# GpSimd's constant operand: a row of 256 int32 in place of one int32 read with a step of zero

## The chip, the core and the metric

One NeuronCore of a Trainium2 chip runs the whole kernel. The metric is device time in microseconds (us) for one execution. The engines are called as the profile calls them: PE (TensorE; PEld its weight loads), DVE (VectorE), ACT (ScalarE), POOL (GpSimd) and SP (SyncE, which issues most of the DMAs).

## What is computed

One input x of 2048 tokens with 512 columns goes through two attention blocks of 32 heads with 16 columns each, and a gate mixes their outputs:

```python
x = A_x
g = _sigmoid((x * gate_w).sum(-1, keepdims=True))
a = _A_ref(x, A_wqkv, A_wo)     # softmax(q k^T / 4) v, then @ wo
b = _B_ref(x, B_wqkv, B_wo)     # phi(q) (phi(k)^T v) / (phi(q) sum phi(k)), then @ wo
return g * a + (1 - g) * b
```

Block A is the large part: 32 heads x 2048 x 2048 scores, an exponential of each, and a product with v (P@V) that also sums the exponentials. All of it in bf16 with fp32 accumulation, output 2048 x 512 in bf16.

## The kernel before, in words

**Tiling.** Eight heads share the 128 partitions (`NT8` = 4 groups of heads). A round is one group of heads, one chunk of 512 queries and every second head of the group, 32 rounds in all. A round has 64 units, 4 heads x 16 blocks of 128 keys; a unit is one head's scores for 128 keys x 512 queries: a matmul Q·K into a PSUM bank of 128 x 512, an exponential of it, and a P@V matmul into the bank in which the round accumulates. PE's matmuls are recorded in `pe_macro` (L685), so they all carry that line.

**Two ways to an exponential.** Most units take the first: ACT's exponential of two banks at a time from PSUM into the tile PT (L2063). The others are *claimed* (`claim`) by DVE and POOL. DVE evicts a claimed bank with one instruction (L1565), a maximum and an addition with int16 output; the integer is the bit pattern of an fp16 number that rises with the score roughly as the exponential does. To make it accurate, the kernel uses three such patterns, the second and third shifted by a constant (`STEPS` = 0, 342, 683), and lets P@V add them with weights that are multiplied into copies of v. The patterns lie in the tile DP: `NB` = 13 buffers of `NTU` = 2048 int16 a partition, each of them `NTRI` = 4 claimed units.

**The add.** When four units fill a buffer, `try_close` takes a free buffer for each of the two shifted patterns and pushes an addition of the constant. It has two forms. On DVE it is L1606: 2048 int16 plus a scalar. On POOL it is L1609: a TENSOR_TENSOR over int32, two int16 patterns at a time, 1024 int32 a partition; the second operand is the tile `steps`, which holds the constant twice in two int16, that is in one int32, for each of the two shifts:

```python
steps = SB([128, 4], I16, "step")                                             # L312
for z in range(1, NG4):                                                       # L734
    op(PO, lambda z=z: nc.gpsimd.memset(steps[:, 2 * z - 2:2 * z], STEPS[z]), writes=[r_step], dur=0.1)
...
DP[:, i2, 0:n].bitcast(I32), y, steps[:, 2 * z - 2:2 * z].bitcast(I32).to_broadcast([128, n // 2]), ALU.add))   # L1610
```

`to_broadcast` gives that one int32 a step of zero, so it is read 1024 times. The two memsets (L735) stand among POOL's first instructions, behind the zeroing of `warm` (L733) and ahead of the identity (L736, L737), the masks (L730, L740, L743) and the clearing of v's copies and of smaller tiles (L760 to L764).

**What sets the order.** The program is laid out ahead of time: a planner keeps a clock for each engine, estimates the duration of each operation (`POOL_ADD` = 1.97 us for L1609, `POOL_TT` = 1.3 us for L1294), and decides which additions go to POOL and which to DVE, and where each instruction stands in its engine's list (`pump`, `pool_go`, `emit_item_op`). The lists are then fixed; on the chip each engine works its list in order and waits on semaphores. `_emit` gives every POOL instruction one wait beyond its data: on the last DVE instruction ahead of it that has no PSUM operand, since the two engines get in each other's way at SBUF. Among those DVE instructions are L1606, L973 (a clamp of the exponentials of block B's features), L925 (the weighted copies of v), L1279 (reciprocals of the sums) and L1253 (a check of their range). POOL's only other repeated instruction is L1294, the product of P@V's output with the reciprocals, 128 x 512 fp32 twice in, bf16 out.

**Around it.** At the start a load of x is transposed by PE (L692) with the identity of L737, and the first projections follow; block B's steps and the output projection are spread between the rounds. At the end, once ACT has no more units, PE finishes the last P@V matmuls and the projection of the last 512 rows (L2154 to L2168), and the rows are stored.

Of the kernel before, what the change touches and what calls it, by code (L numbers as in the profile page):

```python
# [9 lines left out]
ALU = mybir.AluOpType  # L10
# [3 lines left out]
I32 = mybir.dt.int32  # L14
I16 = mybir.dt.int16
# [15 lines left out]
STEPS = (0, 342, 683)  # L31
# [173 lines left out]
def d_sb(n, rate=1.0):  # L205
    return 0.15 + n * 1.042e-3 * rate


def d_act(n):
    return ACT_END + n * 8.34e-4  # L210


def bass_gated_mix__mha_block__linear_attn_block__prompt_kernel(
# [33 lines left out]
    with ExitStack() as es:  # L247
        _cnt = [0]

        def SB(shape, dt, name):  # L250
            _cnt[0] += 1
            return es.enter_context(nc.sbuf_tensor(f"{name}_{_cnt[0]}", list(shape), dt))

        def SEM(name):
            return es.enter_context(nc.semaphore(name))
# [47 lines left out]
        DP = SB([128, NB, NTU], BF16, "DP")  # L303
# [5 lines left out]
        rbc = SB([128, 512], FP32, "rbc")  # L309
        dev = SB([128, 2, 128], FP32, "dev")  # L310
        flag = SB([128, 1], I32, "flag")
        steps = SB([128, 4], I16, "step")  # L312
        epool = SB([128, 2, 512], BF16, "epool")
        KVbd = SB([128, NCC, 128], BF16, "KVbd")
        Zsel = SB([128, NCC, 8], BF16, "Zsel")
# [38 lines left out]
        PO = _Eng("pool", SEM("s_pool"))  # L354
# [43 lines left out]
        r_step = R("step")  # L398
# [111 lines left out]
        def settle(reads, writes):  # L510

            while True:
                hit = None
                for it in items:
                    for k, o in enumerate(it.ops):
                        if conflicts(o, reads, writes):
                            hit = it
                            break
                    if hit:
                        break  # L520
                if hit is None:
                    return
                while True:
                    other = blocker(hit, hit.ops[0][1], hit.ops[0][2])
                    if other is None:
                        break
                    hit = other
                emit_item_op(hit)

        def _emit(E, fn, reads, writes, dur, issue=None, inc=True):  # L530
            st = est_start(E, reads, writes)
            deps = _deps_for(reads, writes)
            if E is PO:
                deps.append(port_ev[0])
            ev = E.add(fn, deps, inc=inc)
            if E is DV and not any(res in r_bank for res in reads):
                port_free[0] = st + dur - 0.03
                port_ev[0] = ev
            _record(E, ev, reads, writes)
            E.t = st + (issue if issue is not None else max(0.05, dur - 0.08))  # L540
            for res in reads:
                res.tr = max(res.tr, st + dur)
            for res in writes:
                res.tw = st + dur
                res.we = E
            return ev

        def op(E, fn, reads=(), writes=(), dur=0.2, issue=None):
            settle(reads, writes)
            return _emit(E, fn, reads, writes, dur, issue)  # L550

        def push(prio, ops):

            iseq[0] += 1
            it = _Item(prio, iseq[0], ops)
            items.append(it)
            for o in it.ops:
                for res in o[1]:
                    res.pend += 1
                for res in o[2]:  # L560
                    res.pend += 1
                    res.pw += 1
# [8 lines left out]
        def pump(now, look=0.25):  # L571
            try_close()
            pool_go()
            while items and DV.t <= now + look:
                best = None
                for it in items:
                    o = it.ops[0]
                    if len(o) == 6 or blocked(it, o[1], o[2]):
                        continue
                    if len(o) > 6 and not due_now(it) and PO.t < DV.t + POOL_WAIT:  # L580
                        continue
                    st = est_start(DV, o[1], o[2])
                    wait = st - DV.t
                    key = (wait > (WAIT_BANK if it.prio <= 1 else 0.12), -1 if it is boost[0] else it.prio, st, it.seq)
                    if best is None or key < best[0]:
                        best = (key, it, st)
                if best is None:
                    return
                if best[2] > now + look + WAIT_BANK:
                    return  # L590
                emit_item_op(best[1], False)
                pool_go()
# [98 lines left out]
        def f_tr(o, i):  # L691
# [12 lines left out]
           dur=1.6)  # L704
# [9 lines left out]
        for t in range(1, NQC):  # L714
            for cc in range(NCD):
                dma(xT[:, cc, 512 * t:512 * (t + 1)], x2[512 * t:512 * (t + 1), 128 * cc:128 * (cc + 1)], semXT[cc][t],
                    writes=[r_xT[cc][t]], total_after=16, transpose=True, E=SP, lands=5.5)
# [14 lines left out]

        op(PO, lambda: nc.gpsimd.memset(warm[:], 0.0), writes=[r_warm])  # L733
        for z in range(1, NG4):  # L734
            op(PO, lambda z=z: nc.gpsimd.memset(steps[:, 2 * z - 2:2 * z], STEPS[z]), writes=[r_step], dur=0.1)  # L735
        op(PO, lambda: nc.gpsimd.memset(identb[:], 0.0), writes=[r_ident])  # L736
        op(PO, lambda: nc.gpsimd.affine_select(out=identb[:], in_=identb[:], compare_op=ALU.not_equal,  # L737
                                               fill=1.0, base=0, pattern=[[-1, 128]], channel_multiplier=1),
# [805 lines left out]
        def free_buffers():  # L1544

            used = [e[3] for e in pv_pending]
            held_ = [c[0] for c in (tri[0], *closing) if c is not None]
            free = [i for i in range(NB) if i not in held_ and not any(x.pend or x in used for x in r_DP[i])]
            free.sort(key=lambda i: max(x.tr for x in r_DP[i]))
            return free  # L1550
# [21 lines left out]
        def add_products(i, z, k, r, u):  # L1572
            pv_pending.append((r, u, [(DP[:, i, 512 * k:512 * (k + 1)].bitcast(F16), z)], r_DP[i][k], Fraction(1, NG4)))

        def close_tri():
            if tri[0] is not None:
                closing.append((*tri[0], []))
                tri[0] = None
            try_close()
# [7 lines left out]
        def try_close():  # L1587

            while closing:
                i, us, zs = closing[0]  # L1590
                z = len(zs) + 1
                if z == NG4:
                    closing.popleft()
                    continue
                free = free_buffers()
                early = us[0][0] > acc_round[0]
                if len(free) < (LAZY if early else 1):
                    return False
                if not zs and sum(1 for it in items if it.prio == 3) >= (EARLY_ADDS if early else MOST_ADDS):
                    return False  # L1600
                i2 = free[0]
                zs.append(i2)
                n = 512 * len(us)
                y = DP[:, i, 0:n].bitcast(I16)
                mine_, out_ = r_DP[i][0:len(us)], r_DP[i2][0:len(us)]
                ops = (lambda z=z, i2=i2, y=y, n=n: nc.vector.tensor_single_scalar(DP[:, i2, 0:n].bitcast(I16), y, STEPS[z], ALU.add),  # L1606
                       mine_, out_, d_sb(n, 0.25), None)
                if n == NTU:
                    ops = (ops[0], mine_ + [r_step], out_, ops[3], None, POOL_ADD, lambda z=z, i2=i2, y=DP[:, i, 0:n].bitcast(I32), n=n: nc.gpsimd.tensor_tensor(  # L1609
                        DP[:, i2, 0:n].bitcast(I32), y, steps[:, 2 * z - 2:2 * z].bitcast(I32).to_broadcast([128, n // 2]), ALU.add))  # L1610
                push(3, [ops])
                of_round[iseq[0]] = us[0][0]
                for k, (r, u) in enumerate(us):
                    add_products(i2, z, k, r, u)
            return True
# [364 lines left out]
        while True:  # L1980
# [72 lines left out]
            for c, eb in extras:  # L2053
# [4 lines left out]
                     dur=QK_T, mac=0.053 * len(fns), mode="rows")  # L2058
            for c, eb in extras:
                claim(c[0], c[1], eb, True, in_group=True)  # L2060
            STATS["claims %d+%d" % (len(us), len(extras))] = STATS.get("claims %d+%d" % (len(us), len(extras)), 0) + 1
            n = 512 * len(us)
# [3 lines left out]
               dur=d_act(n), issue=0.055 + n * 8.34e-4)  # L2066
# [59 lines left out]
        while pv_pending:  # L2126
            if not pv_step(PE.t, force=True):
# [9 lines left out]
                 writes=[r_bank[tbank]], dur=0.3)  # L2137
# [8 lines left out]
           writes=[r_bad], dur=0.25)  # L2146
# [15 lines left out]
        for k in range(NPRE):  # L2162
# [6 lines left out]
            if k == 0:  # L2169
# [4 lines left out]
                         writes=[r_bank[tbank]], dur=0.1)  # L2174
# [47 lines left out]
        for t8 in range(NT8):  # L2222
# [11 lines left out]
            for qc in range(NQC):  # L2234
                for h in range(8):
# [6 lines left out]
                    for k in range(4):  # L2242
# [4 lines left out]
                           writes=[r_sm] + r_rdB)  # L2247
# [16 lines left out]
        for tb in range(NTB):  # L2264
            s3 = tb % NOUTT
            pe_macro(out_fns(bank_ap(tb % 4), tb, order_out), reads=[r_OT[t][tb // 4] for t in range(NT8)] + [r_OBT[tb], r_woA, r_woB],
                     writes=[r_bank[tb % 4]])
# [87 lines left out]
```

## Time and profile before

| what | value |
|---|---|
| median of 3 runs | 675.63 us (675.6 to 675.94) |
| the profiled execution, its own time | 675.2 us |
| its span, first to last instruction | 673.4 us |
| busy in the span: PE, DVE, ACT, POOL | 655.0, 576.0, 660.0, 550.8 us |
| ACT exponentials L2063 | 675, 648.1 us |
| DVE evictions L1565 of claimed units | 654, 433.0 us |
| POOL additions L1609 | 278, 527.0 us, mean 1925 ns |
| DVE additions L1606 | 50, 33.4 us |

How to read it: a row of groups names the line, the engine, the operation, the tiles written and read with their shapes, the count, the busy time and the mean duration, and then the idle time of the engine just before these instructions with what ended it. A row of waits reads "who <- for whom: us in total, times, longest". A row of windows lists for each engine the busy time in that stretch. A row of the timeline starts with the start time and the duration of a run of like instructions. Busy PE is no measure of PE's speed, since matmuls are pipelined.

### The profile page before, as it was taken

The page shows a single profiled execution, that of the slowest core. Times are in us where ns is not written, and L with a number is a line of the kernel's source. Part 1 is how long each engine was busy: PE and PEld are TensorE (multiplying, and loading weights), DVE is VectorE, ACT ScalarE, POOL GpSimd, SP SyncE. Part 2 cuts the span into 40 slices and gives each one's busy share as a digit, 9 for nine tenths or more (in the row PEclk, how much of TensorE's full clock was granted, in tenths as well). Part 3 has the DMA queues.
Part 4 walks back from the last instruction along what each step waited for, and adds up shares of the span by engine and source line. Part 5 has one row for each costly group of instructions (what it writes and reads, how often), then busy time and mean ns, then how long its engine had stood idle before and what let it go on. Part 6 is the DMA issues. An engine that isn't in the chain of part 4 may idle for free.

```text
span 673.4 us, 19207 instructions
## 1 busy us (share of the span) xinstructions
PE 655.0 (97%) x8078; PEld 200.1 (30%) x8080; DVE 576.0 (86%) x968; ACT 660.0 (98%) x715; POOL 550.8 (82%) x311
## 2 busy tenths in 40 slices
PE   8999999999999999999999999999999999999997
PEld 4322223333223232333222323323322222222223
DVE  4589889889887886888988998999889998989894
ACT  6999999999999999999999999999999999999995
POOL 5098889887889997788986999778788888898883
PEclk9999999999999999999999999999999999999999
DMA  9900101001010021101001010010211401010011
GB/s 221 252 3 12 24 2 31 6 11 27 1 35 2 18 50 35 32 2 29 7 10 35 10 41 11 16 29 13 46 26 24 52 25 42 10 44 24 20 41 44
DMA packets 44816, 22.96 MB, mean 34 GB/s; under 512 B 33976, under 2 KB 40568, under 8 KB 44728
## 3 DMA queue, kind: packets, MB, share of 16 engines
q1 hardware_dynamic: 42712, 20.12, 13.5%
q10 hardware_dynamic: 2016, 1.57, 0.9%
q8 instruction: 66, 1.08, 0.7%
q14 instruction: 22, 0.18, 0.1%
HBM read 8.00 MB, written 2.10 MB: 15 GB/s over the span
## 4 chain that ended last, share of the span: by engine, by line
ACT 95%; PE 4%; DMA 1%; DVE 1%; issue 0%; ACTq 0%
ACT PT L2063 92%; PE ps L685 3%; ACT epool L970 2%; DMA PT<-in_A_x_dram 1%; DVE DP L2165 0%; DVE xT L1909 0%; PE ps L692 0%; DVE KT L859 0%; DVE DP L2170 0%; DVE flag L2175 0%; ACT eg L954 0%; ACTq L2278 0%
## 5 line engine op out<-in xcount | busy, mean ns | idle before, releaser
L2063 ACT ACTIVATE PT<-ps 128x1024 bf16<-128x1024 f32 (+1 forms) x675 | 648.1, 1155 | 0.7 <-PE ps L685 0.5
L1609 POOL TENSOR_TENSOR DP<-DP,step 128x1024 int32<-128x1024 int32 x278 | 527.0, 1925 | 99.1 <-DVE DP L1565 27.6
L1565 DVE TENSOR_SCALAR DP<-ps 128x512 int16<-128x512 f32 x654 | 433.0, 685 | 69.1 <-PE ps L685 62.9
L685 PE MATMUL ps<-Qpad,KT 32*128 32x512 bf16 x2048 | 264.6, 384 | 10.0 <-ACT PT L2063 4.7
L685 PE MATMUL ps<-DP,Vaug 128*32 128x512 f16 x1949 | 206.8, 384 | 1.6 <-DVE oraw L1306 0.7
L685 PE MATMUL ps<-PT,Vaug 128*32 128x512 bf16 x1384 | 174.3, 384 | 0.6 <-DVE Vaug L914 0.5
L685 PEld LDWEIGHTS ps<-Qpad,KT 32*128 32x128 bf16 x2048 | 66.6, 91 | 269.9 <-ACT PT L2063 242.9
L685 PEld LDWEIGHTS ps<-DP,Vaug 128*32 128x32 bf16 x1949 | 49.7, 94 | 66.2 <-issue 41.1
L685 PEld LDWEIGHTS ps<-PT,Vaug 128*32 128x32 bf16 x1384 | 42.1, 95 | 46.7 <-issue 36.7
L685 PE MATMUL ps<-warm 128*32 128x512 bf16 (+1 forms) x272 | 46.7, 387 | 1.1 <-POOL step L735 1.1
L1606 DVE TENSOR_SCALAR DP<-DP 128x2048 int16<-128x2048 int16 (+1 forms) x50 | 33.4, 696 | 0.0
L685 PE MATMUL ps<-xT,wA 128*32 128x512 bf16 x432 | 32.6, 384 | 0.0
L1294 POOL TENSOR_TENSOR OT<-oraw,rbc 128x512 bf16<-128x512 f32 x12 | 15.6, 1302 | 11.3 <-DVE DP L1606 5.4
L970 ACT ACTIVATE epool<-ps 128x512 bf16<-128x512 f32 x32 | 23.4, 731 | 0.0
L1306 DVE COPY oraw<-ps 128x512 f32<-128x512 f32 x31 | 21.2, 682 | 0.7 <-PE ps L685 0.6
L685 PE MATMUL ps<-xT,wB 128*32 128x512 bf16 x256 | 19.7, 384 | 0.0
L685 PE MATMUL ps<-wB,xT 128*32 128x512 bf16 x256 | 19.3, 384 | 0.0
L685 PE MATMUL ps<-woA,OT 128*32 128x512 bf16 (+1 forms) x226 | 19.1, 384 | 0.0
L975 DVE SCALAR_TENSOR_TENSOR phi<-ps,epool 128x512 bf16<-128x512 f32 x24 | 16.3, 681 | 0.0
L685 PEld LDWEIGHTS ps<-warm 128*32 128x32 bf16 (+1 forms) x272 | 11.6, 98 | 13.8 <-issue 12.1
L859 DVE CAST KT<-ps 128x512 bf16<-128x512 f32 (+1 forms) x16 | 10.7, 667 | 5.2 <-PE ps L685 5.2
L685 PE MATMUL ps<-wA,xT 128*128 128x128 bf16 x192 | 14.9, 220 | 0.0
(106 smaller groups left out, 244.4 us busy)
## 6 DMA issues: line engine op xcount, KB each, us to landing
rbc<-oraw SPq DMA_DIRECT2D x16, 256.0 KB
OT<-in_A_x_dram SPq DMA_DIRECT2D x4, 512.0 KB, 7.1
Qpad<-Qs SPq DMA_DIRECT2D x124, 16.0 KB, 1.8
oraw<-oraw SPq DMA_DIRECT2D x60, 32.0 KB, 1.9
wA<-in_A_wqkv_dram SPq DMA_DIRECT2D x1, 1536.0 KB, 7.7
wB<-in_B_wqkv_dram SPq DMA_DIRECT2D x1, 1536.0 KB, 8.6
out_dram<-outt SPq DMA_DIRECT2D x12, 128.0 KB, 1.7
phi<-in_A_x_dram ACTq DMA_DIRECT2D x3, 256.0 KB, 6.1
```

The source lines that it names most:

```text
L685: return lambda: nc.tensor.matmul(o, lhsT=l, rhs=r, start=start, stop=stop, skip_group_check=sg)
L859: push(1, [(lambda: nc.vector.tensor_copy(KT[:, par, c0:c1], src), [r_bank[b]], [r_KT[par][t]], d_psum(n), None)])
L970: op(AC, lambda: nc.scalar.activation(epool[:, s, :], bank_ap(b), ACT.Exp), reads=[r_bank[b]], writes=[r_e[s]], dur=0.6, issue=0.48)
L975: (lambda: nc.vector.scalar_tensor_tensor(out=dst, in0=bank_ap(b), scalar=0.0, in1=epool[:, s, :], op0=ALU.max, op1=ALU.add), [r_bank[b], ...
L1294: push(1, [(lambda: (nc.gpsimd if on_pool else nc.vector).tensor_tensor(OT[:, t8, 512 * qc:512 * (qc + 1)], oraw[:, 0, :], rbc[:], ALU.mul ...
L1306: push(0, [(lambda: nc.vector.tensor_copy(oraw[:, half, :], acc), [r_acc], [r_oraw[half]], d_psum(512), evicted)])
L1565: push(0 if in_group else 1, [(lambda: nc.vector.tensor_scalar(DP[:, i, 512 * k:512 * (k + 1)].bitcast(I16), bank_ap(b), FRAC - Y_BIAS4, Y ...
L1606: ops = (lambda z=z, i2=i2, y=y, n=n: nc.vector.tensor_single_scalar(DP[:, i2, 0:n].bitcast(I16), y, STEPS[z], ALU.add), mine_, out_, d_sb ...
L1609: ops = (ops[0], mine_ + [r_step], out_, ops[3], None, POOL_ADD, lambda z=z, i2=i2, y=DP[:, i, 0:n].bitcast(I32), n=n: nc.gpsimd.tensor_te ...
L2063: op(AC, lambda p0=p0, b0=b0, n=n: nc.scalar.activation(PT[:, 512 * p0:512 * p0 + n], ps[:, 512 * b0:512 * b0 + n], ACT.Exp, scale=LN2 / F ...
```

## The change

The tile `steps` grows from 2 int16 to 512 int16 a partition for each of the two constants (`STEP_W` = 512), and the memsets fill all of it. The addition on POOL then reads 256 int32 of that row one after the other and begins again, four times for the 1024 elements; the patterns that it reads and writes are the same elements in the same order, only written as 4 x 256. Nothing else is edited; the form on DVE and the planner's costs stay.

```diff
-        steps = SB([128, 4], I16, "step")
+        STEP_W = 512
+        steps = SB([128, 2 * STEP_W], I16, "step")
...
-            op(PO, lambda z=z: nc.gpsimd.memset(steps[:, 2 * z - 2:2 * z], STEPS[z]), writes=[r_step], dur=0.1)
+            op(PO, lambda z=z: nc.gpsimd.memset(steps[:, STEP_W * (z - 1):STEP_W * z], STEPS[z]), writes=[r_step], dur=0.1)
...
-                        DP[:, i2, 0:n].bitcast(I32), y, steps[:, 2 * z - 2:2 * z].bitcast(I32).to_broadcast([128, n // 2]), ALU.add))
+                        DP[:, i2, 0:n].bitcast(I32).rearrange("p (a b) -> p a b", b=STEP_W // 2), y.rearrange("p (a b) -> p a b", b=STEP_W // 2),
+                        steps[:, STEP_W * (z - 1):STEP_W * z].bitcast(I32).unsqueeze(1).to_broadcast([128, n // STEP_W, STEP_W // 2]), ALU.add))
```

## The prediction

> **What bounds the kernel now.** The page comes first, for the chain that ended last; then the waits of ACT, to see whether that chain has holes; then the windows, to see where each engine stands inside and outside the long stage.
>
> ```profile
> span 673.4 us, 19207 instructions
> PE 655.0 (97%) x8078; PEld 200.1 (30%) x8080; DVE 576.0 (86%) x968; ACT 660.0 (98%) x715; POOL 550.8 (82%) x311
> ...
> ACT 95%; PE 4%; DMA 1%; DVE 1%; issue 0%; ACTq 0%
> ```
>
> ```profile
> ACT xT L1907 <- PE ps L692: 2.8, 1, 2.8
> ...
> ACT PT L2063 <- PE ps L685: 0.5, 1, 0.5
> ```
>
> ```profile
> 0.00:32.50 32.50, 29.74 (x361) 13.15 (x361) 16.44 (x33) 26.12 (x26) 8.64 (x21) 1.00 0.94 244
> 32.50:663.00 630.50, 618.80 (x7601) 182.92 (x7602) 555.03 (x924) 630.48 (x687) 542.16 (x290) 1.00 0.11 23
> 663.00:673.40 10.40, 6.50 (x120) 4.03 (x118) 4.58 (x13) 3.38 (x5) 0.00 (x0) 0.99 0.17 56
> ```
>
> The windows list PE, PEld, DVE, ACT, POOL. From 32.5 to 663 us ACT is busy 630.48 of 630.50 us, and its exponentials (L2063) waited for anything once, for 0.5 us. ACT sets the time; there is nothing in that stage to win by speeding up another engine. POOL, whose instruction the change touches, works 542.16 us of the same 630.50: it is not the bound, and has 88.3 us of idle time before it becomes one.
>
> **The edited add.** Its durations (minimum/median/maximum), a stretch of three on end, and POOL's waits:
>
> ```profile
> L1609 POOL TENSOR_TENSOR DP<-DP,step x278: 1886/1892/2397, 32.5 to 660.6; 128x1024 int32<-128x1024 int32 x139
> ```
>
> ```profile
> 639.87 5.59 POOL L1609 TENSOR_TENSOR DP<-DP,step 128x1024 int32<-128x1024 int32 x3
> ```
>
> ```profile
> POOL DP L1609 <- DVE DP L1565: 27.6, 5, 22.2
> POOL DP L1609 <- DVE epool L973: 21.7, 29, 1.4
> POOL DP L1609 <- DVE DP L1606: 14.9, 11, 2.0
> POOL DP L1609 <- DVE Vaug L925: 7.9, 5, 1.8
> ```
>
> ```profile
> L973 DVE TENSOR_SCALAR epool<-epool 128x512 bf16<-128x512 bf16 x32 | 10.3, 323 | 1.9 <-ACT epool L970 0.5
> ```
>
> There are 278 adds, nearly all at 1.89 us; on end they follow each other every (5.59 - 1.89) / 2 = 1.85 us. The instructions, their count, order and waits stay as they are: the planner's cost POOL_ADD (1.97) is not edited, so neither is anything laid out by it. What changes is how the second operand is read: now one int32 a partition, 1024 times over; afterwards 256 int32 in a row, the row four times. So the question is one price: what the add costs when its second operand moves too.
>
> No row has that add. **From above**, the only other two-input instruction on POOL reads two moving operands:
>
> ```profile
> L1294 POOL TENSOR_TENSOR OT<-oraw,rbc x12: 1265/1274/1602, 77.2 to 530.2; 128x512 bf16<-128x512 f32 x12
> ```
>
> ```profile
> L737 POOL TENSOR_SCALAR_AFFINE_SELECT identb<-identb 128x128 bf16<-128x128 bf16 x1 | 0.3, 294 | 0.2 <-POOL identb L736 0.2
> ...
> L730 POOL TENSOR_SCALAR_AFFINE_SELECT maskK<-maskK 128x8 f32<-128x8 f32 x2 | 0.4, 194 | 0.1
> ```
>
> It takes 1265 ns at best for 512 elements, so twice that, 2.53 us, for 1024 without any fixed part. The fixed part of an instruction that reads and writes I take from the two selects: 8 elements in 194 ns and 128 in 294 is 0.83 ns an element and 187 ns fixed. Then L1294 pays (1265 - 187) / 512 = 2.11 ns an element and the present add (1886 - 187) / 1024 = 1.66. **From below**, the second stream may cost nothing more (1.89 us stays), or less: a row on end could be fetched several elements at a time. Nothing in the rows excludes that; a loss of one whole stream's share, half of 1.66 ns, would bring it to 0.187 + 1024 x 0.83 / 1000 = 1.04 us. I take the row that it is nearest to in what is read, two moving operands of 4 bytes: 0.187 + 1024 x 2.11 / 1000 = 2.35 us, that is 2.35 - 1.89 = +0.46 us. What speaks against it: L1294 multiplies floats and writes bf16, and its higher rate may come from that.
>
> [...]
>
> **What of it lies on the path.** 278 x 0.46 = 128 us more of POOL's work, against 88 us idle. The idle time isn't all free. Every POOL instruction is made to wait for the last DVE instruction ahead of it that works from SBUF, and the waits above are those: 29 on L973, 0.75 us each, of which L973 itself is 0.32 us; 11 on L1606, 1.35 us each, of which L1606 is some 0.7 (its row stands below). That part comes back however late POOL is; the other half, in which POOL stood ready before the DVE instruction had begun, takes up lateness. I count half, 44 us, as absorbed. The rest is on the path: a late add holds the P@V matmuls that read it, PE works in order, the scores behind them come late, and ACT runs dry. The cover is thin, since PE already meets the adds at their end:
>
> ```profile
> PEld ps L685 <- POOL DP L1609: 10.2, 37, 0.5
> ...
> PE ps L685 <- POOL DP L1609: 0.3, 2, 0.2
> ```
>
> ```profile
> L1606 DVE TENSOR_SCALAR DP<-DP x50: 415/686/1752, 51.2 to 663.9; 128x2048 int16<-128x2048 int16 x48, 128x1024 int16<-128x1024 int16 x2
> ```
>
> On DVE, the SBUF instructions that meet a running add stretch with it (L1606 from 686 to as much as 1752 ns); behind them in DVE's queue stand the evictions L1565, for which PE's banks wait. This is not added: it is part of the same lateness. **Sum: 675.2 (the profiled execution; 1.8 us lie around its span) + 128 - 44 = 759 us.** The runs shown have a median of 675.63, so the sum against them differs by 0.4 us, which is nothing beside it.
>
> **The two memsets of the constant** grow from 2 to 512 int16 a partition.
>
> ```profile
> L764 POOL MEMSET Osb<- 128x512 bf16 x1 | 0.5, 534 | 0.0
> ...
> L735 POOL MEMSET step<- 128x2 int16 x2 | 0.2, 100 | 0.1
> ```
>
> ```profile
> 1.61 0.29 POOL L737 TENSOR_SCALAR_AFFINE_SELECT identb<-identb 128x128 bf16<-128x128 bf16 x1 [0.23 <-POOL identb L736]
> ...
> 2.02 0.46 POOL L730 TENSOR_SCALAR_AFFINE_SELECT maskK<-maskK 128x8 f32<-128x8 f32 x2
> ...
> 3.72 0.10 DVE L758 TENSOR_REDUCE maskQ<-maskK 128x1 f32<-128x4 f32 x1
> ...
> 4.92 0.90 PEld L692 LDWEIGHTS ps<-identb,PT 128*128 128x128 bf16 x16 [0.72 <-DMA PT<-in_A_x_dram]
> ...
> 32.52 3.74 POOL L1609 TENSOR_TENSOR DP<-DP,step 128x1024 int32<-128x1024 int32 x2 [22.21 <-DVE DP L1565]
> ```
>
> By L764 that is 2 x (534 - 100) = 0.87 us on POOL, hidden: identb would be ready at 1.90 + 0.87 = 2.77 us, while PE waits for a load until 4.92; the mask at 3.35, before DVE reads it at 3.72; and all of POOL's start lies ahead of 22.21 us of idle time. Without this cover it would be 0.9 us. The tile grows by 2040 bytes a partition and moves those behind it; no row prices an address, and I take nothing.
>
> **Rivals.** About 0.2% (1.35 us) is what a measurement can tell from no change.
>
> *A, the same price.* A row read on end costs a port no more than one element again and again; the higher rate of L1294 belongs to its floats. For it: L1609's spread of 1886 to 1892 looks like a fixed pace. Then 675.2 us, chance 0.25. [...]
>
> *B, a small price.* The restart of the row, or a quarter of the gap between the two rates: 0.03 to 0.2 us an add. At 0.1 us POOL gets 28 us more work, less than the 44 it can take up, but not always where it has them: the 39 places at which PE already waits give 39 x 0.1 = 4 us. At 0.2 us it is 56 - 44 = 12 us. So 676 to 690, say 680; chance 0.15, of which 0.13 slower by over 0.2%.
>
> *C, the other side.* The row is fetched several elements at a time, and the add falls below 1.89 us, to 1.04 at best. Then the waits of PE on POOL, 10.2 + 0.3 us, go. ACT stays full, so this shows in the time only where PE and not ACT ends the chain, which is 4% of it:
>
> ```profile
> 648.19 11.91 PE ps L685 x160
> 660.25 3.40 PE ps L685 x24
> ```
>
> In proportion that is 0.04 x 10.5 = 0.4 us, 674.8 us. It passes 0.2% (under 674.3) only if over 0.9 us of those waits lie after 648 us. Chance 0.13, of which 0.05 faster.
>
> *The forecast,* 759 us, has a chance of 0.47: below it bounds by half of the extra price (0.23 us: 64 - 44 = 20, 695 us), above by 2.53 us an add (178 - 44 = 134, 809 us). Its own range is 695 to 809.
>
> **How the numbers follow.** Slower: 0.47 + 0.13 = 0.60. Same: 0.25 + 0.02 + 0.08 = 0.35. Faster: 0.05. The range goes from 674.3, which takes in A, B and most of C, to 775, which cuts off what lies above the forecast's middle (some 0.12) and leaves with the faster cases less than 0.2 out.
>
> **What will show it.** Right: L1609 at 2.3 to 2.4 us, POOL over 95% busy between 32 us and the end, its waits on L973 and L1606 down by half, PE waiting on POOL for tens of us, ACT on PE, and the chain of waits through L1609 in place of L2063. L735 at about 0.5 us without anyone waiting. Wrong at the price: L1609 still at 1.89 (A), or below (C), with the rest of the page as before. Wrong at the path: L1609 at 2.35 and ACT still full, which would mean that buffers of P take up far more lateness than 44 us.

## The result, and the profile after

The changed kernel takes 765.4 us (median of 3 runs, 760.05 to 765.58) against 675.63: 1.130 times as long, 95% interval 1.128 to 1.132. The profiled execution took 765.58 us, 1.8 us of it around its span, as before. The page and the windows (PE, PEld, DVE, ACT, POOL) of the changed kernel, in which every line number behind the new one is higher by one or two (the add is L1610, the exponentials L2065):

```profile
span 763.8 us, 19209 instructions
PE 676.1 (89%) x8080; PEld 202.0 (26%) x8080; DVE 619.4 (81%) x968; ACT 677.3 (89%) x715; POOL 680.0 (89%) x311
...
POOL 50%; PE 27%; DVE 14%; ACT 6%; issue 2%; POOLq 0%; DVEq 0%; ACTq 0%
...
L1610 POOL TENSOR_TENSOR DP<-DP,step 128x1024 int32<-128x1024 int32 x278 | 655.5, 2392 | 66.5 <-DVE DP L1566 27.6
```

```profile
32.50:753.00 720.50, 639.87 (x7610) 184.49 (x7602) 598.26 (x925) 648.35 (x688) 669.50 (x290) 0.97 0.10 21
```

The chain that ended last (the work followed back, step by step, from the last instruction to what released it) was 95% ACT; it is now half POOL and 6% ACT. ACT, busy all but 0.02 us of the long stage before, idles 72 of 720.5 us. The add, its waits and who waits for it:

```profile
L1610 POOL TENSOR_TENSOR DP<-DP,step x278: 2337/2360/2836, 32.8 to 751.4; 128x1024 int32<-128x1024 int32 x139
```

```profile
PEld ps L686 <- POOL DP L1610: 104.5, 140, 2.0
...
ACT PT L2065 <- PE ps L686: 70.2, 116, 4.5
PE ps L686 <- POOL DP L1610: 60.2, 100, 1.5
...
POOL DP L1610 <- DVE DP L1607: 12.4, 11, 1.8
...
POOL DP L1610 <- DVE epool L974: 7.8, 29, 0.6
```

The loss is in the add: 655.5 - 527.0 = 128.5 us more of it. POOL's idle time ahead of the add and of the other product fell from 99.1 + 11.3 to 66.5 + 6.4 us, by 37.5. The difference, 91.0 us, is the span's growth, 763.8 - 673.4 = 90.4, but for 0.6 us. An engine's busy and idle times always add up to the span, so this is bookkeeping and proves nothing by itself; that the row is the cause is left to the experiments. The three runs of this one kernel lie 5.5 us apart, so a term of a few us can't be read from one of them.

How a late add reaches ACT, in the timeline of the changed kernel:

```profile
649.21 11.63 POOL L1610 TENSOR_TENSOR DP<-DP,step 128x1024 int32<-128x1024 int32 x5
...
656.27 0.12 PEld L686 LDWEIGHTS ps<-DP,Vaug 128*32 128x32 bf16 x8 [0.89 <-POOL DP L1610]
...
656.82 0.39 PE L686 MATMUL ps<-Qpad,KT 32*128 32x512 bf16 x4
657.27 1.02 ACT L2065 ACTIVATE PT<-ps 128x1024 bf16<-128x1024 f32 x1 [0.38 <-PE ps L686]
...
658.58 0.12 PEld L686 LDWEIGHTS ps<-DP,Vaug 128*32 128x32 bf16 x8 [1.66 <-POOL DP L1610]
```

POOL adds without a break, PE's weight loads for the P@V matmuls that read the sums wait for it (0.89 us, then 1.66), the scores behind them start late, and the exponential at 657.27 has waited 0.38 us for them.

### The profile page after: what moved, and what is told of

It is laid out like the page before. It is cut to its first block, busy times and chain, and to the rows that moved or that the text cites. A ratio compares the mean times of both kernels' runs of the same rounds, so it can differ in the third digit from the quotient of the medians.

```text
span 763.8 us, 19209 instructions
## 1 busy us (share of the span) xinstructions
PE 676.1 (89%) x8080; PEld 202.0 (26%) x8080; DVE 619.4 (81%) x968; ACT 677.3 (89%) x715; POOL 680.0 (89%) x311
## 4 chain that ended last, share of the span: by engine, by line
POOL 50%; PE 27%; DVE 14%; ACT 6%; issue 2%; POOLq 0%; DVEq 0%; ACTq 0%
POOL DP L1610 49%; PE ps L686 27%; ACT PT L2065 6%; DVE DP L1566 5%; DVE DP L1607 3%; DVE epool L974 2%; DVE OT L1295 1%; POOL OT L1295 1%; POOLq L2307 0%; DVE rdB L1076 0%; ACT epool L971 0%; DVE rdB L1077 0%; DVE gom L959 0%; DVE dev L1254 0%; DVE DP L2167 0%
## 5 line engine op out<-in xcount | busy, mean ns | idle before, releaser
L2065 ACT ACTIVATE PT<-ps 128x1024 bf16<-128x1024 f32 (+1 forms) x675 | 662.0, 1068 | 72.8 <-PE ps L686 70.2
L1610 POOL TENSOR_TENSOR DP<-DP,step 128x1024 int32<-128x1024 int32 x278 | 655.5, 2392 | 66.5 <-DVE DP L1566 27.6
L1566 DVE TENSOR_SCALAR DP<-ps 128x512 int16<-128x512 f32 x654 | 434.1, 684 | 117.0 <-PE ps L686 111.6
L686 PE MATMUL ps<-Qpad,KT 32*128 32x512 bf16 x2048 | 269.8, 392 | 13.5 <-DVE OB L1010 4.4
L686 PE MATMUL ps<-DP,Vaug 128*32 128x512 f16 x1949 | 215.9, 397 | 61.3 <-POOL DP L1610 55.9
L686 PE MATMUL ps<-PT,Vaug 128*32 128x512 bf16 x1384 | 178.9, 393 | 5.8 <-POOL DP L1610 3.5
L1607 DVE TENSOR_SCALAR DP<-DP 128x2048 int16<-128x2048 int16 (+1 forms) x50 | 47.0, 968 | 0.0
L974 DVE TENSOR_SCALAR epool<-epool 128x512 bf16<-128x512 bf16 x32 | 26.5, 827 | 0.3
L971 ACT ACTIVATE epool<-ps 128x512 bf16<-128x512 f32 x32 | 20.0, 624 | 0.0
## 6 DMA issues: line engine op xcount, KB each, us to landing
wB<-in_B_wqkv_dram SPq DMA_DIRECT2D x1, 1536.0 KB, 10.3
```

Of the source, the lines that this page charges most:

```text
L686: return lambda: nc.tensor.matmul(o, lhsT=l, rhs=r, start=start, stop=stop, skip_group_check=sg)
L971: op(AC, lambda: nc.scalar.activation(epool[:, s, :], bank_ap(b), ACT.Exp), reads=[r_bank[b]], writes=[r_e[s]], dur=0.6, issue=0.48)
L974: (lambda: nc.vector.tensor_scalar(epool[:, s, :], epool[:, s, :], 1.0, 1e-6, op0=ALU.min, op1=ALU.add), [r_e[s]], [r_e[s]], 0.29, None),
L1566: push(0 if in_group else 1, [(lambda: nc.vector.tensor_scalar(DP[:, i, 512 * k:512 * (k + 1)].bitcast(I16), bank_ap(b), FRAC - Y_BIAS4, Y ...
L2065: op(AC, lambda p0=p0, b0=b0, n=n: nc.scalar.activation(PT[:, 512 * p0:512 * p0 + n], ps[:, 512 * b0:512 * b0 + n], ACT.Exp, scale=LN2 / F ...
```

## The experiments

Theory S: a second operand that moves through memory costs the add 0.47 us, whatever its type, and the rest follows from POOL being late. Its rivals are the row's new starts (R), the larger tile, which moves those behind it (place), and, for the price of the other product, its floats. The later runs narrow theory S and try a theory F, by which the second operand is fetched in pieces of 16 bytes. All but three of the runs were executed once: the runs with every step zero, with the row in half of the adds, and with the new plan have several executions.

**Rows of 512, twice an add** (`STEP_W` = 1024).

```diff
-        STEP_W = 512
+        STEP_W = 1024
```

> The changed kernel with rows of 512 int32 in place of 256, so that the row begins again twice an add and not four times. Theory S (the second operand moves, and a second moving stream costs the add 0.47 us): the add stays at 2.36 us and the time near 765 us. Theory R (each new start of the row costs about 0.12 us): two starts instead of four, the add at 2.13 us, POOL 64 us shorter, the time near 700 us.

```profile
L1610 POOL TENSOR_TENSOR DP<-DP,step x278: 2336/2360/2827, 33.0 to 752.5; 128x1024 int32<-128x1024 int32 x139
```

The median add takes 2360 ns as with rows of 256, and the time was 766.69 us. R falls.

**The same tile, memsets and pattern, every step zero.**

```diff
-                        steps[:, STEP_W * (z - 1):STEP_W * z].bitcast(I32).unsqueeze(1).to_broadcast(...)
+                        steps[:, STEP_W * (z - 1):STEP_W * (z - 1) + 2].bitcast(I32).unsqueeze(1).to_broadcast(...)
```

> The changed kernel with its large tile, its memsets of 512 int16 and its pattern of 4 x 256, but every step of the second operand is zero. Theory S: the add at 1.89 us and the time of the kernel before, 675.6 us within 0.2%, memsets included. Theory R or a theory of place (the larger tile moves the tiles behind it): the add at 2.36 us and 765 us.

```profile
L1610 POOL TENSOR_TENSOR DP<-DP,step x278: 1884/1892/2397, 32.3 to 660.4; 128x1024 int32<-128x1024 int32 x139
```

The time was 675.83 us, 1.0004 of the kernel before (0.9994 to 1.0013). The tile, its place, the memsets and the 4 x 256 form together cost nothing that can be measured; the whole loss is in reading the row.

**The row in one of the two shifted patterns.**

```diff
-  ... STEP_W * (z - 1):STEP_W * z] ...
+  ... STEP_W * (z - 1):STEP_W * (z - 1) + (STEP_W if moves else 2)] ...     # moves = (z == 1)
```

> The row is read on end in the first of the two shifted patterns only, in half of the adds (139); the other half has a step of zero in the same tile. POOL gets 139 x 0.47 = 65 us more work. If half of its 88 us of idle time takes up lateness, as the prediction had it, 675.6 + 65 - 44 = 697 us. If all of it does, 676 us; if nothing does, 741 us; if the loss is in proportion to the adds, 720 us.

```profile
L1610 POOL TENSOR_TENSOR DP<-DP,step 128x1024 int32<-128x1024 int32 x278 | 596.5, 2177 | 65.4 <-DVE DP L1566 24.4 <-DVE DP L1607 11.9 <-DVE epool L974 10.2
L1295 POOL TENSOR_TENSOR OT<-oraw,rbc 128x512 bf16<-128x512 f32 x12 | 15.6, 1298 | 7.5 <-DVE DP L1607 5.1 <-DVE OB L1099 1.3 <-DVE Vaug L926 1.1
```

The time was 708.3 us, 1.051 of before (1.047 to 1.056), between the 697 and the 720 us expected. By their durations POOL has 151 of the first additions and 127 of the second, so its extra work was 596.5 - 527.0 = 69.5 us, not 65; with it, half of the idle time would make 701 us. Idle time gave back 110.4 - 72.9 = 37.5 us, the same as with the row in every add; the span grew by 705.0 - 673.4 = 31.6. So the idle time takes up a fixed amount, already used up at half the extra work, and from there a microsecond on POOL costs one: from half to full the adds grow by 59.0 us and the span by 58.8. That these agree so closely is partly luck, since they are two single executions: the four of this kernel range from 706.38 to 713.16 us. The two shorter ones had PE's granted clock at 0.999, the two longer ones at 0.985 and 0.983; that the clock is what made them longer wasn't tried.

**The other product with a second operand that stands still** (in the kernel before; it multiplies by the wrong numbers).

```diff
-                    OT[:, t8, 512 * qc:512 * (qc + 1)], oraw[:, 0, :], rbc[:], ALU.mult),
+                    OT[:, t8, 512 * qc:512 * (qc + 1)], oraw[:, 0, :], rbc[:, 0:1].to_broadcast([128, 512]), ALU.mult),
```

> The kernel before, with the other POOL product, of floats (line 1294, 12 times), reading one element of its second operand with a step of zero in place of 512 on end: it multiplies by the wrong numbers. Theory S: its duration falls from 1.27 us to 0.187 + 512 x 1.66 ns = 1.04 us, since only one stream moves. Rival (its rate belongs to floats and the bf16 output): it stays at 1.27 us. The time stays at 675 us either way.

```profile
L1294 POOL TENSOR_TENSOR OT<-oraw,rbc x12: 1034/1039/1352, 76.9 to 529.7; 128x512 bf16<-128x512 f32 x12
```

The product took 1.04 us in place of 1.27, and the kernel 674.91 us. The higher rate of that row came from its second stream, not from its floats: the row that the prediction leaned on was the right one.

**Short rows of 8 and of 16 bytes** (`STEP_W` = 4 and 8).

> The changed kernel with a row of 2 int32 (8 bytes), read 512 times over: the second operand moves from element to element but stays in the same 8 bytes. If any step other than zero costs the price: the add at 2.36 us and 765 us, as after. If the price is for fetching new bytes: the add at 1.89 us and 675.6 us. If new starts of a row cost anything, 512 of them show it: over 2.36 us.

> The same with a row of 4 int32 (16 bytes), read 256 times over. If the second operand is fetched anew for every 8 bytes: the add at 2.36 us and 765 us, whatever the row of 2 does. If it is fetched anew for every 16 bytes and the row lies in one such piece: 1.89 us and 675.6 us.

```profile
L1610 POOL TENSOR_TENSOR DP<-DP,step x278: 1881/1892/2397, 32.7 to 661.1; 128x1024 int32<-128x1024 int32 x139
```

```profile
L1610 POOL TENSOR_TENSOR DP<-DP,step x278: 1883/1892/2396, 32.8 to 661.3; 128x1024 int32<-128x1024 int32 x139
```

The first is of the row of 2, the second of the row of 4. Both cost what one element costs (675.79 and 675.94 us). New starts are free, 512 of them too, and a step other than zero is no price by itself.

**The pattern added to itself** (kernel before; wrong exponentials).

```diff
-  ... steps[:, 2 * z - 2:2 * z].bitcast(I32).to_broadcast([128, n // 2]), ALU.add))
+  ... y, ALU.add))
```

> The kernel before, with the pattern itself as second operand in place of the constant, read straight through 1024 elements in one dimension: it adds the pattern to itself and computes wrong exponentials. No row, no new start, the small tile of before. If a second stream that moves costs the price by itself: the add at 2.36 us and 765 us. If the price hangs on a second place in memory that is read by turns with the first, the same addresses in both could cost less: between 1.89 and 2.36 us.

```profile
L1609 POOL TENSOR_TENSOR DP<-DP x278: 1884/1891/2397, 32.6 to 661.1; 128x1024 int32<-128x1024 int32 x139
```

The add took 1.89 us, though both operands move through 4 KB. The time of 7354 us says nothing of the add: at its end the kernel checks the range of the sums and, as they are out of it here, runs its second, general program, whose lines (L2246 to L2254) then fill the trace. Theory S in its first form falls: two moving streams are cheap if they are at the same addresses. With the rows of 8 and 16 bytes, what is left to carry the price is a second operand that moves over more than 16 bytes of another place. Whether the engine reads the pattern twice here or only once, the run doesn't show.

**Rows of 32 and 64 bytes, and steps of 8 and 16 bytes.** The last two read every second or fourth int32 of a longer row; the edit of the run with 16 bytes, in which the patterns are cut into rows of `ROW` likewise:

```diff
-        STEP_W = 512
+        STEP_W = 1024; ROW = 128          # 256 with a step of 2
...
+  ... .bitcast(I32).rearrange("p (b c) -> p b c", c=4)[:, :, 0].unsqueeze(1).to_broadcast([128, n // 2 // ROW, ROW]), ALU.add))
```

> The changed kernel with a row of 8 int32 (32 bytes), read 128 times over. Theory F (the second operand is fetched in pieces of 16 bytes, and each new piece costs 0.47 us / 256 = 1.8 ns): two pieces by turns, a new one every 4 elements as in a long row, so the add at 2.36 us and 765 us. Rival M (several pieces are held, and only a row too long for them is fetched again): 1.89 us and 675.6 us.

> The same with a row of 16 int32 (64 bytes), read 64 times over. Theory F: the add at 2.36 us and 765 us. Rival M: still 1.89 us if 64 bytes are held, otherwise 2.36 us.

> The changed kernel with a row of 256 int32 at a step of two (8 bytes) in a tile twice as long, so that 1024 elements meet 512 pieces of 16 bytes in place of 256. Theory F: 1.89 + 512 x 1.8 ns = 2.83 us, and 675.6 + 278 x 0.94 - 44 = 893 us. [...]

> A row of 128 int32 at a step of four (16 bytes), read 8 times over: a new piece for every element. Theory F: 1.89 + 1024 x 1.8 ns = 3.77 us, and 675.6 + 278 x 1.88 - 44 = 1154 us. Rival (the price doesn't depend on the step): 2.36 us and 765 us.

The add in the row of 8, the row of 16, the step of 8 bytes and the step of 16 bytes:

```profile
L1610 POOL TENSOR_TENSOR DP<-DP,step x278: 2343/2363/2842, 32.2 to 745.2; 128x1024 int32<-128x1024 int32 x139
```

```profile
L1610 POOL TENSOR_TENSOR DP<-DP,step x278: 2338/2359/2818, 33.2 to 748.2; 128x1024 int32<-128x1024 int32 x139
```

```profile
L1610 POOL TENSOR_TENSOR DP<-DP,step x278: 2366/2399/2860, 32.6 to 757.8; 128x1024 int32<-128x1024 int32 x139
```

```profile
L1610 POOL TENSOR_TENSOR DP<-DP,step x278: 2848/2893/3366, 32.8 to 893.3; 128x1024 int32<-128x1024 int32 x139
```

The times were 759.48, 762.51, 772.06 and 908.09 us. The price sets in whole between a row of 16 and one of 32 bytes, as F has it, and M falls. But it doesn't grow with the number of 16-byte pieces: twice as many add 0.04 us where F wanted 0.47, four times as many 0.53 where F wanted 1.41. F falls as a price list. What inside the engine makes it a flat 0.47 us up to steps of 8 bytes, and 1.0 us at 16, stays open; how the short rows lie against 16-byte boundaries wasn't tried either.

The step of 16 bytes also tries POOL's idle time at twice the extra work:

```profile
L1610 POOL TENSOR_TENSOR DP<-DP,step 128x1024 int32<-128x1024 int32 x278 | 803.4, 2934 | 61.0 <-DVE DP L1566 22.0 <-DVE DP L1607 14.8 <-DVE epool L974 9.8
L1295 POOL TENSOR_TENSOR OT<-oraw,rbc 128x512 bf16<-128x512 f32 x12 | 15.6, 1300 | 5.6 <-DVE DP L1607 4.5 <-DVE Vaug L926 1.1
```

The adds grow by 803.4 - 527.0 = 276.4 us, the idle time gives back 110.4 - 66.6 = 43.8, and the span grows by 906.3 - 673.4 = 232.9. In the runs with the row of 512, the row of 8, the row of 16 and the step of 8 bytes, the same working gives 38.2, 45.2, 41.3 and 44.1 us. So at half, whole and double the extra work the idle time gave back about 40 us, 37.5 to 45.2.

**The plan made for the new price.**

```diff
-        POOL_ADD = 1.97
+        POOL_ADD = 2.44
```

> The changed kernel with the planner told of the new price (its cost of the add 2.44 us in place of 1.97, the same 2% above the measured mean), so that it lays the work out anew: fewer adds on POOL, more on DVE, where one takes 0.69 us. If the loss comes from a plan that no longer fits: POOL has 630 - 88 - 16 = 526 us for adds, 220 of them, 58 more on DVE add 40 us to its 555 of 630; about 690 us. If the loss is POOL's work itself: it stays above 740 us.

```profile
span 690.1 us, 19342 instructions
PE 671.4 (97%) x8183; PEld 206.3 (30%) x8183; DVE 591.1 (86%) x990; ACT 673.2 (98%) x716; POOL 523.9 (76%) x242
...
ACT 71%; PE 22%; POOL 3%; DVE 3%; issue 1%; ACTq 0%; POOLq 0%
...
L1610 POOL TENSOR_TENSOR DP<-DP,step 128x1024 int32<-128x1024 int32 x209 | 498.4, 2412 | 135.7 <-DVE DP L1607 72.2
L1566 DVE TENSOR_SCALAR DP<-ps 128x512 int16<-128x512 f32 x623 | 414.6, 687 | 68.1 <-PE ps L686 64.0
```

The time was 691.78 us, 1.024 of before (1.022 to 1.026). With the costlier add still in it, the kernel gets back 765.4 - 691.8 = 74 of 90 us: POOL does 209 additions in place of 278 and DVE 103 in place of 50, 31 units fewer are claimed (623 for 654), and ACT, busy 673.2 us in place of 660.0, holds 71% of the chain and is the bound again. Most of the loss was a plan whose price for one instruction had become wrong; 16 us is what POOL's slower add costs a plan that knows of it. None of these versions beats the kernel before.

## Why the prediction was right, point by point

**The price of the add**: 2.35 us forecast, 2.36 measured, by the same route as forecast: the fixed 187 ns and the rate of the row with two moving operands. The other product with a still operand shows that the reason was right too, and it lets the fixed part be checked, which came from two unlike instructions: its shortest 512 elements (1034 ns) and the shortest 1024 of the add before (1886) leave 182 ns fixed, and those with the moving operand, 1265 and 2337, leave 193. The pattern added to itself and the short rows show that "two moving operands" was too wide a wording. What spoke against the price, that L1294's higher rate may come from its floats and its bf16 output, is settled by the same product: it is one of floats with bf16 output, and the still operand took it from 1.27 to 1.04 us. Rival A had the row cost no more than one element again and again, and the runs show otherwise: the add takes 2.36 us at a step of 4 bytes, 2.40 at 8 and 2.89 at 16, and 1.89 with an operand that stays in place, 0.47 us less than with the row.

**The path**: 278 x 0.46 = 128 us was 128.5. Absorbed idle time, 44 by halving, was 37.5 in the profiled execution, which is the gap between 759 and its 765.58. But another execution of the same kernel took 760.05 us, and the runs at other prices gave back up to 45.2 us, so 44 is within what the runs differ by. That the halving came out is in part luck: of the two waits that it was argued from, L973's shrank by more than half (21.7 to 7.8 us), but L1606's hardly (14.9 to 12.4). These two gave 16.4 us; the other 21 came from waits that the prediction doesn't count, the most from the one on L1279 (the reciprocals), which fell from 7.1 to 1.4 us. POOL ended 93% busy in its stage (669.50 of 720.50), not over 95. A part of the path was named as no addition of its own and showed itself plainly: DVE's instructions that meet POOL. DVE is busy 43.4 us more than before (619.4 for 576.0); the 50 additions of L1607 (L1606 before) take 47.0 us in place of 33.4, and the 32 clamps of L974 (L973 before) 26.5 in place of 10.3. DVE holds 14% of the chain, and what that alone costs wasn't tried apart from POOL's lateness. In the changed kernel, DVE, POOL, PE and ACT around 290 us:

```profile
288.77 6.05 DVE L1607 TENSOR_SCALAR DP<-DP 128x2048 int16<-128x2048 int16 x1
```

```profile
284.94 9.33 POOL L1610 TENSOR_TENSOR DP<-DP,step 128x1024 int32<-128x1024 int32 x4
```

```profile
296.16 0.61 PE L686 MATMUL ps<-Qpad,KT 32*128 32x512 bf16 x4 [4.37 <-DVE OB L1010]
```

```profile
296.82 1.02 ACT L2065 ACTIVATE PT<-ps 128x1024 bf16<-128x1024 f32 x1 [4.50 <-PE ps L686]
```

The DVE addition, 0.68 us in the median, starts while the second of these four POOL adds runs and ends 0.55 us after the last of them, 6.05 us after its start. Behind it stand the evictions of PE's banks, among them L1010 (a copy of block B's output), for which PE waits 4.37 us, and ACT then 4.50.

**The memsets**: 0.87 us forecast, hidden. They took 527 ns each, 0.85 us more together, and the run with every step zero, which keeps them, is at 1.0004. **The chain and the waits** came out as listed: L1610 in the chain, ACT waiting for PE 70.2 us, PE and its weight loads (which overlap: busy 676.1 and 202.0 us in a span of 763.8) for the add 60.2 and 104.5.

## What to carry to other kernels

Read the idle time of an engine before its price is changed, and ask how much of it comes back however late it is: here the 88 us of POOL's idle time in the long stage held only some 40 us of slack, and past that the engine, 86% busy, passed nearly every microsecond on (58.8 us of 59.0 from the row in half of the adds to the row in all). Where a plan is laid out by a table of costs, an edit that changes the price of an instruction belongs into the table with it; that alone was worth 74 of the 90 us. And a price that no row shows is best taken from the row that is nearest in what it reads, not in its arithmetic: here that gave 2.35 us for a measured 2.36.

## What the runs showed of the hardware that was not expected

- A second operand of a POOL addition of 1024 int32 costs nothing extra while it stays within 8 or 16 bytes (1.89 us) or reads the addresses of the first (1.89), 0.47 us once its row has 32 bytes or more (2.36 for rows of 32, 64, 1024 and 2048 bytes), and 1.00 us at a step of 16 bytes (2.89). The jump lies between a step of 8 bytes (2.40 us, 0.04 more than on end) and one of 16 (0.53 more than on end).
- A DVE addition from SBUF that started during a run of POOL adds took 6.05 us, where the median is 0.68, and ended only behind the last add of the run (the rows around 290 us above). The evictions from PSUM did not stretch: 685 ns in the mean before (L1565), 684 in the changed kernel (L1566).
- PE's granted clock, 1.00 in the kernel before, fell in some stretches of the changed kernel. Two windows of it, and the step of the chain that lies there:

```profile
228.70:242.30 13.60, 11.80 (x122) 3.15 (x122) 6.66 (x11) 9.95 (x12) 13.60 (x7) 0.70 0.01 2
242.30:255.90 13.60, 13.39 (x132) 3.85 (x126) 9.99 (x17) 11.98 (x13) 13.60 (x7) 0.79 0.03 7
```

```profile
233.68 15.11 PE ps L686 x110
```

The clock stands behind POOL's busy time: 0.70 and 0.79. What makes it fall isn't shown: from 326.4 to 333.2 us PE is busy for 5.14 of 6.80 us, a smaller share than in either window, at a clock of 1.00. POOL was busy throughout both windows, but the chain runs through PE there, so what the low clock cost can't be read from them. Runs with an add of the same price differ by some 7 us (759.48 with the row of 8, 766.69 with the row of 512), with mean clocks of 0.980 and 0.964; the row of 16, with 762.51 at 0.971, lies between them, but the changed kernel itself took 765.4 at 0.975. Whether the clock is the reason wasn't tried, and a part of the 90 us may be its own.
